# A fused attention, expert and gated-unit kernel: the attention stage issued from one table of finer steps in a new order, a shorter chain for the first expert's last rows, and an earlier first gather

## The chip, the cores and the metric

The kernel runs on one core of a Trainium2 chip. The metric is device time in microseconds (us) for one launch. Five engines work side by side, each through its own instructions in order: TensorE (PE, matrix products; its weight loads are shown apart as PEld), VectorE (DVE), ScalarE (ACT), GpSimd (POOL), and SyncE (SP), which here only issues DMA transfers. POOL and ACT issue some DMA transfers too. An engine waits on semaphores that other engines or transfers set. SBUF is the memory on the core, PSUM the one that PE writes.

## The reference

Three stages follow each other; inputs are float32.

```python
# 1 attention: a linear recurrence with a complex decay, 2 batches x 8 heads x 768 steps x 48
mag = sqrt(a_re**2 + a_im**2); scale = minimum(mag, 0.999) / (mag + 1e-6)
for t in range(S):
    S_re, S_im = (ar*S_re - ai*S_im) + outer(k_t, v_t), ar*S_im + ai*S_re
    y_t = q_t @ S_re
# 2 experts: 1536 tokens x 384, 8 experts of width 1024, each token to its best expert
e = argmax(x @ w_gate); disp[e, count[e]] = x[i]      # in token order, up to a capacity
y = relu(disp[e] @ w1[e]) @ w2[e];  out[i] = gate_w[i] * y[e, pos[i]]
# 3 gated unit of width 1536 behind an RMS norm
xn = x / rms * g;  out = (silu(xn @ w_gate) * (xn @ w_val)) @ w_out
```

## The kernel before

**Attention.** The 12 chunks of 128 time steps (6 for each batch) are called c = 0 to 11 (`LAST` = 11); two neighbouring chunks form a group gi, since their decays are worked out together. For a group, ACT and DVE turn the gates into log magnitudes and angles (`squares`, `logs_1` to `logs_4`, `angles_1` to `angles_4`), with PE summing them over time (`sums`, `angles_2`, `turns`). The logarithms and the sines need two different tables of ACT, so a table load (`ACT_TABLE_LOAD`) stands at each change. For a chunk, `decays` makes the factors `R` and sends their last row to DRAM (`ends`); `ends_in` reads it back as `re`. `scaled` multiplies keys and queries with `R` (tile `kqr`), `frame` turns them by the angle (tiles `K` and `Q`, on DVE), `flip` transposes them on PE and copies them out of PSUM (`KT`, `QT`), `scores` makes half of the heads' score matrices (`ap`) and masks them on DVE (`AT`), `end_decay` transposes `re` on PE (`rp`), `state_up` and `state` carry the recurrent state (`up`, `z`, `st`), `outputs` makes `yp` and `yT`, and `route_1` makes the rows of x and the expert logits (`xb`, `lg_all`).

**Routing.** `choice` finds the best expert, `route_2` and `route_3` a row's place in its expert (`rk`, `slot_all`), and `dispatch` is an indirect DMA from POOL that scatters 128 rows into `disp`. The first expert's input is read back before the last two chunks have been scattered: their rows are added on PE with a matrix of ones (`put`), which DVE makes from `rk` and `mine`. The result, `hi_first` and `lo_first`, feeds the first product of the experts (`hp`).

**Experts.** Weights come in 64 pieces, 8 an expert; the loop has 64 steps n, one a piece, and at step n `ahead(n)` loads piece n + 8 and splits piece n + 4 into a high and a low half (ACT `hi`, DVE `lo`). Weights of the gated unit are loaded and converted in the same loop. The dictionary `more_at` says what is issued besides at a step: the routing table's arithmetic at 1 to 9, twelve scatters of 128 table rows each into `packed` (10, 13, ..., 43), its read back into `meta_in` (46), and the first group of the gated unit: four gathers of 128 rows out of `ybuf` (50), four sums of squares on ACT (`jk`, 53 to 56), the root (57), the scaling on DVE (58), and three transposes on PE (`mxp`, 61 to 63). An expert's results go to `ybuf` at the first step of the next one.

**What sets the order.** `InOrder` wraps each engine so that instructions keep the order in which the Python code calls them. In the attention stage this order is a list of calls for the first chunk and the function `chunk` for the others. Loads of SP stand in the same order. An engine therefore waits at the first instruction that isn't ready, whatever stands behind it.

Of the kernel before, what the change touches and what calls it, by code (L numbers as in the profile page):

```python
# [43 lines left out]
def tile_kernel(ctx: ExitStack, tc: tile.TileContext, q, k, v, a_re, a_im, gates, keys, vals, wg, w1, w2, cap, m_gate, m_val, m_out, rms_g, out, dbg=None):  # L44
# [270 lines left out]
    with ExitStack() as actx:  # L315
# [36 lines left out]

        def tiles(gi):
# [12 lines left out]
        def logs_1(gi, x=ALL):  # L366
            d = gd[gi]
            ea.activation(d["tB"][:, x], d["tA"][:, x], AF.Ln)
            ea.activation(d["tA"][:, x], d["tB"][:, x], AF.Exp, scale=0.5)
            ea.activation(d["l2"][:, x], d["tA"][:, x], AF.Ln, bias=b_eps)  # L370

        def logs_2(gi, x=ALL):
            d = gd[gi]
            ev.scalar_tensor_tensor(d["tB"][:, x], d["tB"][:, x], C_MIN, d["tB"][:, x], ALU.min, ALU.add)
            ev.scalar_tensor_tensor(d["th"][:, x], d["ar"][:, x], 0.0, d["tA"][:, x], ALU.max, ALU.add)
            ev.scalar_tensor_tensor(d["l2"][:, x], d["l2"][:, x], -2.0, d["tB"][:, x], ALU.mult, ALU.add)

        def logs_3(gi, x=ALL):
            d = gd[gi]
            ea.activation(d["th"][:, x], d["th"][:, x], AF.Ln)  # L380
            ea.activation(d["th"][:, x], d["th"][:, x], AF.Exp, scale=-1.0)

        def logs_4(gi, x=ALL, e=None):
            d = gd[gi]
            (e or eg).tensor_tensor(d["th"][:, x], d["ai"][:, x], d["th"][:, x], ALU.mult)
            if 1 < gi < len(groups) - 2:
                load(gi + 2, ["g"])

        def sums(gi, js=range(GM)):
            for j in js:  # L390
                c = groups[gi][j]
                L = ps_cs.tile([P, H, D], F32, tag="cs", name=f"L_{c}")
                et.matmul(f2(L), tri, f2(gd[gi]["l2"][:, j]), start=True, stop=True)
                cd[c]["L"] = L

        def decays(gi, js=range(GM)):
            cs = [groups[gi][j] for j in js]
            for c in cs:
                R = cd[c]["R"] = ch.tile([P, 2, H, D], F32, tag="R", name=f"R_{c}", bufs=4)
                ea.activation(R[:, 0], cd[c]["L"], AF.Exp, scale=-0.5)  # L400
                ea.activation(R[:, 1], cd[c]["L"], AF.Exp, scale=0.5)
                sp.dma_start(ends[c:c + 1], R[P - 1:P, 1])

# [7 lines left out]
        def angles_1(gi, x=ALL):  # L411
            ea.activation(gd[gi]["th"][:, x], gd[gi]["th"][:, x], AF.Arctan)

        def angles_2(gi, j):
            c = groups[gi][j]
# [3 lines left out]
        def turns(gi, j):  # L419

            d, c = gd[gi], groups[gi][j]
# [8 lines left out]
        def angles_3(gi, x=ALL):  # L430
# [3 lines left out]
            ev.tensor_scalar(d["ab"][:, x].bitcast(U32), d["th"][:, x].bitcast(U32), 0x7FFFFFFF, None, ALU.bitwise_and)  # L434

        def angles_4(gi, x=ALL):
# [3 lines left out]
            ea.activation(d["rot"][:, x, :, 1], d["th"][:, x], AF.Sin, scale=-TWO_PI)  # L440
            ea.activation(d["rot"][:, x, :, 0], d["ab"][:, x], AF.Sin, scale=-TWO_PI, bias=b_hpi)

        def scaled(c):

            if c > LAST:
                return
# [16 lines left out]
        def flip(c, hh):  # L463
# [4 lines left out]
            for nm in "KQ":  # L468
# [3 lines left out]
                ea.copy(d[nm + "T"][:, 4 * hh:4 * hh + 4], tp)  # L472
# [11 lines left out]
        def end_decay(c):  # L484
            if c % NC == NC - 1:
                return
# [5 lines left out]
        def state_up(c):  # L492

            d = cd[c]
            if c % NC == NC - 1:
                return
# [3 lines left out]
            return up  # L500

        def state(c, up=None):
            d = cd[c]
            if c % NC == NC - 1:
                return
            if up is None:
                up = state_up(c)
# [7 lines left out]
            eg.tensor_tensor(ns[:, :, :D], z, d["rT"][:, :, None].to_broadcast([2 * D, H, D]), ALU.mult)  # L515
            cd[c + 1]["state"] = ns

        def outputs(c):
# [10 lines left out]
            for ps in (slice(0, 2), slice(2, 4)) if c == LAST else (slice(0, 4),):  # L529
                ea.copy(d["yT"][:, ps], yp[:, ps])  # L530

        def route_1(i, later=False):
# [8 lines left out]
            (ea.copy if i % 2 == 0 or i > LAST - 3 else ev.tensor_copy)(x_t.rearrange("p (q d) -> p q d", q=4), xb[:, :, :2 * D])  # L541
# [3 lines left out]
            if not later:  # L545
                choice(i)

        def choice(i):
            d, lg = cd[i], lg_all[:, i]
            mx = mx_all[:, i]  # L550
            ev.max(mx, lg)
# [6 lines left out]
            if i > LAST - 2:  # L558
                d["mine"] = sm.tile([P, 1], F32, tag="mine", name=f"mine_{i}", bufs=2)
                ev.tensor_scalar(d["mine"], mf, 0.0, None, ALU.is_equal)  # L560

        def route_2(i, first=False):
# [6 lines left out]
            if i > LAST - 2:  # L569
                d["put"] = inp.tile([P, GM, 2, H, D], F32, tag="g", name=f"put_{i}").rearrange("p g r h d -> p (g r h d)")[:, :W]  # L570
                ev.tensor_scalar(d["put"], iota_w, rk[:, 0:1], d["mine"], ALU.is_equal, ALU.mult)
            d["rk"] = rk
            if not first:
                route_3(i)

        def route_3(i):
            d = cd[i]
            rk, oh = d["rk"], oh_all[:, i]
# [10 lines left out]

        def dispatch(i):  # L590
            eg.indirect_dma_start(disp[:, :], bass.IndirectOffsetOnAxis(ap=slot_all[:, i:i + 1], axis=0), cd[i]["x"][:, :], None)

        LN, TRIG = "natural_log_exp_and_others", "trig_and_small"

        def chunk(c, a, l):

            if c == LAST:
                route_2(c - 1)
                dispatch(c - 1)
            end_decay(c)  # L600
            scores(c, 0)
            if c == 1:
                choice(0)
            if l is not None:
                ea.preload_act_table_set(LN)
                logs_1(l)
            elif a is not None and a > 1:
                ea.preload_act_table_set(TRIG)
                angles_1(a)
            frame(c + 1, "kr", "K2")  # L610
            state(c)
            if c + 1 in LOG:
                squares(LOG[c + 1])
            scores(c, 1)
            if 0 < c < LAST:
                route_2(c - 1)
            frame(c + 1, "qr", "Q2")
            if l is not None:
                logs_2(l)
            outputs(c)  # L620
            if a is not None:
                angles_2(a, 0)
                turns(a, 0)
                angles_2(a, 1)
            if c < LAST:
                flip(c + 1, 0)
            if l is not None:
                logs_3(l)
            elif a is not None:
                turns(a, 1)  # L630
                angles_3(a)
            route_1(c)
            if c < LAST:
                flip(c + 1, 1)
            if a is not None:
                angles_4(a)
            if l is not None:
                sums(l)
                decays(l)
                for j in groups[l]:  # L640
                    ends_in(j)
                logs_4(l)
            scaled(c + 2)
            if c < LAST:
                dispatch(c - 1)
            if c == LAST - 1:
                xd_first = inp.tile([P, GM, 2, H, D], F32, tag="kq", name="xd_first")[:, :, 0].rearrange("p g h d -> p g (h d)")
                sp.dma_start(xd_first, disp[0:W, :].rearrange("(s p) d -> p s d", p=P))
                cd[LAST]["xd"] = xd_first

        ea.preload_act_table_set(LN)
        load(0, ["g"], True)
# [39 lines left out]
        u, w = ONE  # L692
        squares(0, u, ev)
        squares(0, w)
        logs_1(0, u)
        logs_2(0, u)
        warm(9)
        sums(0, [0])
        logs_3(0, u)
        logs_4(0, u, ev)  # L700
        logs_1(0, w)
        logs_2(0, w)
        squares(1, ALL, ev)
        logs_3(0, w)
        decays(0, [0])
        logs_1(1)
        logs_4(0, w, ev)
        scaled(0)
        logs_2(1)
        ea.preload_act_table_set(TRIG)  # L710
        angles_1(0, u)
        angles_1(0, w)
        warm(27)
        angles_2(0, 0)
        angles_2(0, 1)
# [472 lines left out]
```

## Time and profile before

| what | value |
|---|---|
| runs, median (lowest to highest) | 546.01 us (544.01 to 546.9), 3 runs |
| the profiled execution's own time | 545.61 us |
| its span, first to last instruction | 543.9 us |
| PE busy | 514.0 us, 95% |
| DVE / ACT / POOL busy | 332.6 / 294.7 / 96.4 us |
| mean granted clock of PE | 0.986 of full speed |

The span is cut into stages by PE's own instructions: the first scores of chunk 1 start at 41.84 us, the first product of the experts at 160.72, the eighth expert at 286.61 and the gated unit at 311.78. A busy PE is not a PE at its peak: matmuls are pipelined and the record of one covers its passage, so that short waits can vanish in it.

### The profile page before, as it was taken

To read this page: it belongs to the slowest core of one execution; us is meant where nothing else is said; L and a number is where in the kernel's file an instruction comes from. 1 tells how busy PE (TensorE), PEld (TensorE's weight loads), DVE (VectorE), ACT (ScalarE), POOL (GpSimd) and SP (SyncE) were. 2 spreads that over 40 slices of the span, in tenths; PEclk is the share of its full clock that TensorE was granted. 3 is DMA by queue.
4 is the path that set the end of the run, shared out by engine and by line. 5 is a ranking of instruction groups with operands and counts; after the bars stand their busy time and mean duration, and the time that the engine had idled before them with its cause. 6 is when DMAs were issued, how large, how long until landed. Compare 5 with 4: busy or idle time off the path is not lost. (4 is left out here: it accounts for less than half of the span.)

```text
span 543.9 us, 8679 instructions
## 1 busy us (share of the span) xinstructions
PE 514.0 (95%) x3298; PEld 454.6 (84%) x3298; DVE 332.6 (61%) x659; ACT 294.7 (54%) x492; POOL 96.4 (18%) x147
## 2 busy tenths in 40 slices
PE   6789998999889999999999799999999999999994
PEld 2467876778779999999998788899988899888894
DVE  4749798797747989898976887751144431333300
ACT  6868697794426776777758465642223421323200
POOL 5022441633800112110020020001400001000011
PEclk9979999999999999999999899999999999999998
DMA  8175714305317989999994252310221100000000
GB/s 302 41 253 179 257 36 152 127 11 164 102 60 242 321 254 289 319 313 305 283 341 140 69 193 87 100 47 30 72 74 29 30 14 30 16 1 0 2 31 33
DMA packets 31579, 72.74 MB, mean 134 GB/s; under 512 B 6750, under 2 KB 13674, under 8 KB 31530
## 3 DMA queue, kind: packets, MB, share of 16 engines
q1 hardware_dynamic: 26538, 61.86, 35.3%
q0 software_dynamic: 2688, 7.10, 3.8%
q10 hardware_dynamic: 2304, 3.15, 1.6%
q8 instruction: 28, 0.46, 0.3%
q14 instruction: 21, 0.17, 0.1%
HBM read 59.87 MB, written 12.23 MB: 133 GB/s over the span
## 5 line engine op out<-in xcount | busy, mean ns | idle before, releaser
L58 DVE TENSOR_TENSOR sg<-vp,sg 128x512 f32<-128x512 f32 x36 | 24.9, 692 | 77.1 <-PE vp L58 75.0
L58 DVE TENSOR_TENSOR lo<-raw,hi 128x768 fp32r<-128x768 f32 x60 | 57.2, 953 | 8.1 <-ACT hi L58 7.5
L58 ACT CAST hi<-raw 128x768 fp32r<-128x768 f32 x64 | 53.2, 835 | 8.1 <-PE op L58 2.7
L58 ACT CAST uh<-sg 128x512 fp32r<-128x512 f32 x36 | 22.3, 620 | 64.8 <-DVE sg L58 60.5
L58 PE MATMUL mop<-oh__3912,uh 128*128 128x384 f32 x144 | 48.7, 338 | 0.0
L58 PE MATMUL mop<-ol__3913,uh 128*128 128x384 f32 x144 | 48.2, 335 | 0.0
L58 PE MATMUL mop<-oh__3912,ul 128*128 128x384 f32 x144 | 48.2, 334 | 0.0
L58 POOL DMA_INDIRECT out<-ot,meta_in x12 | 11.7, 976 | 202.0 <-ACT ot L58 202.0
L58 PE MATMUL op<-hi,hh 128*128 128x384 f32 x128 | 45.6, 356 | 0.0
L58 PE MATMUL op<-hi,hl 128*128 128x384 f32 x128 | 43.6, 341 | 0.2 <-DVE hl L58 0.2
L58 PE MATMUL op<-lo,hh 128*128 128x384 f32 x128 | 43.5, 340 | 0.0
L58 ACT COPY ot<-mop 128x384 f32<-128x384 f32 x12 | 5.8, 481 | 53.1 <-PE mop L58 53.1
L58 DVE TENSOR_TENSOR ul<-sg,uh 128x512 fp32r<-128x512 f32 x36 | 24.8, 689 | 11.9 <-ACT uh L58 11.9
L58 ACT ACTIVATE sg<-gp 128x512 f32<-128x512 f32 x36 | 21.5, 598 | 16.9 <-PE gp L58 16.6
L58 PE MATMUL gp<-mxh,gh 128*128 128x512 f32 x108 | 30.6, 391 | 0.0
L58 PE MATMUL gp<-mxl,gh 128*128 128x512 f32 x108 | 30.4, 389 | 0.0
L58 PE MATMUL gp<-mxh,gl 128*128 128x512 f32 x108 | 30.3, 389 | 0.0
L58 PE MATMUL vp<-mxh,vh 128*128 128x512 f32 x108 | 30.3, 389 | 0.0
L58 PE MATMUL vp<-mxl,vh 128*128 128x512 f32 x108 | 30.3, 389 | 0.0
L58 PE MATMUL vp<-mxh,vl 128*128 128x512 f32 x108 | 30.3, 389 | 0.0
L58 PE MATMUL ap<-QT,KT 96*128 96x128 f32 x192 | 28.0, 291 | 2.3 <-DVE AT L58 1.5
L58 PE MATMUL hp<-xh,hi 128*128 128x256 f32 x168 | 29.5, 283 | 0.5 <-ACT xh L58 0.5
(215 smaller groups left out, 1279.2 us busy)
## 6 DMA issues: line engine op xcount, KB each, us to landing
raw<-in_moe_w SPq DMA_DIRECT2D x64, 384.0 KB
w_g<-in_moe_w_gate SPq DMA_DIRECT2D x9, 512.0 KB
w_v<-in_moe_w_val SPq DMA_DIRECT2D x9, 512.0 KB
w_o<-in_moe_w_out SPq DMA_DIRECT2D x12, 384.0 KB
g<-in_gates SPq DMA_DIRECT2D x5, 768.0 KB
kq<-in_keys SPq DMA_DIRECT2D x5, 768.0 KB
v<-in_vals SPq DMA_DIRECT2D x12, 256.0 KB
disp<-zt SPq DMA_DIRECT2D x4, 768.0 KB
```

The source lines that it names most:

```text
L58: ins = getattr(self.eng, op)(*args, **kw)
```

## The change

The attention stage is now issued from a table, `ORDER`. A step is a name and a chunk or group (`sc.9` is `scaled` for chunk 9; `u` and `w` are the two halves of group 0); an apostrophe puts the step's work on another engine. Against before, `scaled` goes from DVE to POOL for seven chunks (0, 1, 2, 5, 6, 9, 10); four copies to `QT`, three to x and one to `yT` go from ACT to DVE; two state products and one angle product go from POOL to DVE. `act` loads a table of ACT whenever the next function needs the other one. `logs_1` to `logs_3` are cut into single instructions.

```diff
-        def chunk(c, a, l):
-
-            if c == LAST:
-                route_2(c - 1)
-                dispatch(c - 1)
-            end_decay(c)
-            scores(c, 0)
...
-        for c in range(1, B * NC):
-            chunk(c, ANG.get(c), LOG.get(c))
...
+        ORDER = """
...
+            mi.10 d.9 s0.11 s1.11 o.11
+            ch.10 rt.10 x.11' xd.0 d.10 fi.0 mi.11 pi.10 pi.11
+        """
+        for line in ORDER.strip().splitlines():
+            for step in line.split():
+                name, at = step.rstrip("'").split(".")
+                do[name](at, step.endswith("'"))
```

For the last two chunks `mine` gets the place in the first expert from the logits themselves, without the index of the best expert:

```diff
+        def mine(i):
+
+            lg, mx = lg_all[:, i], mx_all[:, i]
+            ev.max(mx, lg)
+            own = sm.tile([P, 1], BF16, tag="own", name=f"own_{i}", bufs=2)
+            ev.tensor_scalar(own, lg[:, 0:1], mx[:, 0:1], None, ALU.is_ge)
+            r0 = ps_r.tile([P, 1], F32, tag="r", name=f"r0_{i}")
+            et.matmul(r0, ones_b, acc_oh[:, 0:1], start=True, stop=False)
+            et.matmul(r0, strict, own, start=False, stop=True)
+            own_f = sm.tile([P, 1], F32, tag="own_f", name=f"own_f_{i}", bufs=2)
+            ev.tensor_copy(own_f, own)
...
+            ev.tensor_scalar(put, iota_w, r0, own_f, ALU.is_equal, ALU.mult)
```

The rest of the last chunk's routing (`choice`, `route_2`) comes behind `lo_first`. In the expert loop the gathers read only the rows of the first five experts, and the steps move:

```diff
-            return g.indirect_dma_start(y, None, ybuf[:, :], bass.IndirectOffsetOnAxis(ap=meta_in[:, i, 0:1], axis=0))
+            return g.indirect_dma_start(y, None, ybuf[:(E - 3) * W, :] if i < TG else ybuf[:, :], bass.IndirectOffsetOnAxis(ap=meta_in[:, i, 0:1], axis=0))
...
+        def first_places():
+
+            ev.tensor_scalar(meta_in[:, :TG, 0], meta_in[:, :TG, 0], (E - 3) * W - 1, None, ALU.min)
+            list(islice(early, TG))
...
-        more_at = {10 + 3 * i: partial(scatter, i) for i in range(NT)}
+        more_at = {10 + 2 * i: partial(scatter, i) for i in range(NT)}
...
-        more_at[46] = read_packed
-        for n, steps in ((50, 4), (53, 1), (54, 1), (55, 1), (56, 1), (57, 1), (58, 1), (61, 1), (62, 1), (63, 1)):
+        more_at[37] = read_packed
+        more_at[42] = first_places
+        for n, steps in ((49, 1), (50, 1), (51, 1), (52, 1), (53, 1), (54, 1), (61, 1), (62, 1), (63, 1)):
```

On PE in the first chunk, before the change, the transpose of the decay's last row (`rp`) stands between the two halves of the scores (`ap_0`, `ap_1`):

```order
L58 MATMUL L_383<-l_1_273,tri 128x384
L58 MATMUL Kp_1_388<-ident,K_0_335 96x128 x4
L58 MATMUL Qp_1_394<-ident,Q_0_337 96x128 x4
L58 MATMUL L_400<-l_1_273,tri 128x384
L58 MATMUL ap_0_431<-QT_369,KT_370 128x128 x4
L58 MATMUL up_437<-v_214,K_0_335 96x48 x8
L58 MATMUL rp_446<-ident,re_357 96x8
L58 MATMUL ap_1_455<-QT_369,KT_370 128x128 x4
```

After it, on PE in the first chunk, the same transpose stands between the first two angle sums (`TH`), ahead of the last six of the 42 filler products (`warm`):

```order
L58 MATMUL TH_327<-th_242,tri_th 128x384
L58 MATMUL rp_335<-ident,re_294 96x8
L58 MATMUL TH_339<-th_242,tri_th 128x384
L58 MATMUL L_344<-l_0_241,tri 128x384
L58 LDWEIGHTS ones_b
```

The transpose and its wait for `re` have moved ahead of the first chunk's scores.

On POOL around chunks 7 and 8 (`th` is an angle product, `st` a state, `sq` a sum of squares, `disp<-x` a dispatch), before:

```order
L58 TENSOR_TENSOR th_996<-g_674,th_996 128x768
L58 DMA disp<-x_1071,slot_all 2176x384
L58 MEMSET st_1248 96x8x16
L58 TENSOR_TENSOR st_1248<-z_1246,rT_1224 96x8x48
L58 TENSOR_TENSOR sq_1251<-sq_1251 128x2x384
L58 DMA disp<-x_1174,slot_all 2176x384
```

On POOL at the same place, after:

```order
L58 TENSOR_TENSOR th_995<-g_674,th_995 128x768
L58 MEMSET st_1255 96x8x16
L58 TENSOR_TENSOR st_1255<-z_1253,rT_1203 96x8x48
L58 TENSOR_TENSOR kqr_1280<-kq_1022,R_1249 128x768
L58 TENSOR_TENSOR sq_1288<-sq_1288 128x2x384
L58 DMA disp<-x_1037,slot_all 2176x384
```

A product `kqr` of 128x768, which was DVE's, has come in, and the dispatch stands behind it.

On ACT in the seventh expert (`yd` its results to `ybuf`, `hh` the first products' high half, `hi` a weight piece, `xh` the next expert's input), before:

```order
L58 ACTIVATE hh_3_3579<-hp_3_3552 128x512
L58 CAST xh_3585<-xp_0_3587 128x256
L58 CAST hi_3609<-raw_3462 128x768
L58 CAST gh<-wf_g_1_3412 128x512
L58 ACTIVATE jk_0_3615,ms_3516<-yt_3515,meta_in 128x384
L58 CAST xh_3585<-xp_1_3617 128x256
```

On ACT in the seventh expert, after:

```order
L58 COPY yd_3489<-op_1_3359 128x384
L58 DMA ybuf<-yd_3489 128x384
L58 ACTIVATE hh_0_3494<-hp_0_3462 128x512
L58 ACTIVATE jk_0_3498,ms_3288<-yt_3287,meta_in 128x384
L58 CAST hi_3524<-raw_3404 128x768
L58 CAST vh<-wf_v_0_3345 128x512
L58 ACTIVATE hh_1_3530<-hp_1_3500 128x512
```

The first use of a gathered tile, `jk_0`, has moved from behind the fourth `hh` of the expert to behind its first.

## Rows read from the trace of the kernel before

**Rows 1.** Busy time by stage: stretch, its length, busy of each engine, clock, DMA share, GB/s.
```profile
0.00:41.84 41.84, 32.27 (x156) 19.24 (x156) 22.74 (x39) 30.77 (x48) 10.12 (x71) 0.92 0.58 203
41.84:160.72 118.88, 109.65 (x1019) 92.81 (x1019) 95.11 (x250) 81.54 (x127) 47.91 (x39) 1.00 0.37 121
160.72:286.61 125.89, 125.52 (x887) 123.89 (x886) 110.21 (x185) 88.47 (x152) 18.80 (x17) 1.00 0.89 289
286.61:311.78 25.17, 21.34 (x133) 19.85 (x133) 19.61 (x34) 16.30 (x31) 0.00 (x0) 0.93 0.32 100
```

**Rows 2.** Timeline of PE from 30.9 us: start, us, engine, operation, idle before.
```profile
30.94 0.22 PE L58 MATMUL rp<-ident,re 8*96 8x8 f32 x1 [1.77 <-DMA re<-ends]
```

**Rows 3.** Timeline of SP's transfers from 14 us; merged rows cover several.
```profile
14.57 10.11 SPq L58 DMA_DIRECT2D ends<-R  x2
...
25.48 2.44 SPq L58 DMA_DIRECT2D re<-ends  x4
```

**Rows 4.** Busy time and clock in two stretches where the clock fell.
```profile
30.00:38.00 8.00, 7.06 (x32) 5.08 (x33) 3.92 (x6) 4.54 (x6) 1.66 (x2) 0.57 0.57 223
303.60:307.60 4.00, 4.00 (x17) 3.90 (x17) 3.96 (x8) 0.42 (x1) 0.00 (x0) 0.57 0.00 0
```

**Rows 5.** Waits of PE from 41.84 to 160.72: us in total, times, longest.
```profile
PE Qp L58 <- DVE Q L58: 2.0, 2, 1.8
PE yp L58 <- DVE end L58: 1.6, 3, 0.7
PE ap L58 <- DVE AT L58: 1.5, 6, 0.3
PE xb L58 <- ACT yT L58: 1.5, 4, 0.6
```

**Rows 6.** Timeline of DVE from 142 us: two products of one shape.
```profile
142.67 2.40 DVE L58 TENSOR_TENSOR K<-kqr,rot 128x768 f32<-128x768 f32 x1
...
146.76 0.95 DVE L58 TENSOR_TENSOR Q<-kqr,rot 128x768 f32<-128x768 f32 x1
```

**Rows 7.** Timeline of POOL from 142 us.
```profile
142.45 4.30 POOL L58 TENSOR_TENSOR lo<-raw,hi 128x768 fp32r<-128x768 f32 x2 [2.23 <-ACT hi L58]
```

**Rows 8.** Groups of DVE and of POOL, 40 to 151: busy us, mean ns, idle.
```profile
L58 DVE TENSOR_TENSOR K<-kqr,rot 128x768 f32<-128x768 f32 x10 | 11.0, 1096 | 2.5 <-ACT rot L58 2.5
L58 DVE TENSOR_TENSOR kqr<-kq,R 128x768 f32<-128x768 f32 x9 | 8.5, 950 | 0.0
...
L58 POOL TENSOR_TENSOR th<-g,th 128x768 f32<-128x768 f32 x4 | 8.0, 1997 | 26.5 <-ACT th L58 26.5
```

**Rows 9.** Timelines of DVE and PE at the end of the attention stage.
```profile
156.68 0.16 DVE L58 FIND_INDEX8 mi<-mx_all,lg_all 128x8 uint32<-128x8 f32 x1
...
157.06 0.23 DVE L58 TENSOR_SCALAR oh_all<-iota,mf 128x8 bf16<-128x8 f32 x1
...
159.51 0.70 PE L58 MATMUL xp_first_at<-put,x 128*128 128x256 f32 x2 [0.52 <-DVE put L58]
```

**Rows 10.** Waits of PE from 286 to 312.
```profile
PE mxp L58 <- issue: 3.1, 1, 3.1
PE hp L58 <- ACT xh L58: 0.5, 1, 0.5
PE op L58 <- DVE hl L58: 0.2, 1, 0.2
```

**Rows 11.** One tile (`packed`): its scatters' ns, first and last start; their landing.
```profile
L58 POOL DMA_INDIRECT packed<-meta,place x12: 966/1094/1642, 181.5 to 245.2; - x12
...
DMA to landing us min/median/max: 4.2/5.3/7.3
```

**Rows 12.** Timelines of SP, POOL and ACT around the first gather.
```profile
264.44 0.39 SPq L58 DMA_DIRECT2D meta_in<-packed  x1
...
279.45 0.99 POOL L58 DMA_INDIRECT yt<-ybuf,meta_in  x1 [33.09 <-DMA raw<-in_moe_w]
...
284.34 0.62 ACT L58 ACTIVATE jk<-yt,meta_in 128x384 f32<-128x384 f32 x1 [4.47 <-DMA yt<-ybuf,meta_in]
```

More of the change, by code (lines that the diff above doesn't have):

```diff
@@ L351, in tile_kernel, with act @@
         ONE = [slice(j, j + 1) for j in range(GM)]
+        LN, TRIG = "natural_log_exp_and_others", "trig_and_small"
+        table = [None]
+        def act(need, out, x, func, **kw):
+            if table[0] != need:
+                ea.preload_act_table_set(need)
+                table[0] = need
+            ea.activation(out, x, func, **kw)
         def tiles(gi):
@@ L385, in logs_4, with sums, decays @@
             (e or eg).tensor_tensor(d["th"][:, x], d["ai"][:, x], d["th"][:, x], ALU.mult)
[L386 to L402, printed above, removed]
+        def sums(c):
+            gi, j = group_of[c]
+            L = cd[c]["L"] = ps_cs.tile([P, H, D], F32, tag="cs", name=f"L_{c}")
+            et.matmul(f2(L), tri, f2(gd[gi]["l2"][:, j]), start=True, stop=True)
+        def decays(c):
+            R = cd[c]["R"] = ch.tile([P, 2, H, D], F32, tag="R", name=f"R_{c}", bufs=4)
+            act(LN, R[:, 0], cd[c]["L"], AF.Exp, scale=-0.5)
+            act(LN, R[:, 1], cd[c]["L"], AF.Exp, scale=0.5)
+            sp.dma_start(ends[c:c + 1], R[P - 1:P, 1])
         def ends_in(c):
@@ L439, in angles_4, with scaled @@
                 d["rot"] = tmp.tile([P, GM, H, 2, D], F32, tag="rot", name=f"rot_{gi}", bufs=2)
[L440 to L446, printed above, removed]
+            act(TRIG, d["rot"][:, x, :, 1], d["th"][:, x], AF.Sin, scale=-TWO_PI)
+            act(TRIG, d["rot"][:, x, :, 0], d["ab"][:, x], AF.Sin, scale=-TWO_PI, bias=b_hpi)
+        def scaled(c, e=None):
             d = cd[c]
@@ L471, in flip @@
                     et.transpose(tp[:, h], d[nm + "2"][:, 4 * hh + h].rearrange("p j d -> p (j d)"), ident)
-                ea.copy(d[nm + "T"][:, 4 * hh:4 * hh + 4], tp)
+                (e.tensor_copy if e is not None and nm == "Q" else ea.copy)(d[nm + "T"][:, 4 * hh:4 * hh + 4], tp)
         def scores(c, hh):
@@ L588, in route_3, with first_in @@
             ev.tensor_tensor(acc_oh, acc_oh, oh, ALU.add)
+        first, xps = [], []
+        def first_in():
+            first.extend(wsp.tile([P, KD, W], F32R, tag=tg, name=f"{tg}_first", bufs=LS + 1) for tg in ("hi", "lo"))
+            xps.extend(p.tile([P, W], F32, tag=tg, name=f"xp_first_{tg}") for p, tg in ((ps_at, "at"), (ps_cs, "cs"), (ps_cs, "cs")))
+            for kk in range(KD):
+                for t in range(2):
+                    et.matmul(xps[kk][:, t * P:(t + 1) * P], cd[LAST]["xd"][:, t, kk * P:(kk + 1) * P], ident, start=t == 0, stop=False)
@@ L590, in dispatch, with put_in @@
+        def put_in(c):
+            for kk in range(KD):
+                et.matmul(xps[kk], cd[c]["x"][:, kk * P:(kk + 1) * P], cd[c]["put"], start=False, stop=c == LAST)
         def dispatch(i):
             eg.indirect_dma_start(disp[:, :], bass.IndirectOffsetOnAxis(ap=slot_all[:, i:i + 1], axis=0), cd[i]["x"][:, :], None)
-        LN, TRIG = "natural_log_exp_and_others", "trig_and_small"
-        def chunk(c, a, l):
-            if c == LAST:
-                route_2(c - 1)
-                dispatch(c - 1)
-            end_decay(c)
-            scores(c, 0)
[L602 to L649, printed above, removed]
@@ new lines, in xd_in, with of_group, of_group_on @@
+        def xd_in():
+            xd = cd[LAST]["xd"] = inp.tile([P, GM, 2, H, D], F32, tag="kq", name="xd_first")[:, :, 0].rearrange("p g h d -> p g (h d)")
+            sp.dma_start(xd, disp[0:W, :].rearrange("(s p) d -> p s d", p=P))
+        def of_group(f, *more, **kw):
+            return lambda at, o: f(int(at[0]), {"u": ONE[0], "w": ONE[1]}.get(at[1:], ALL), *more, **kw)
+        def of_group_on(f, usual, other):
+            return lambda at, o: f(int(at[0]), {"u": ONE[0], "w": ONE[1]}.get(at[1:], ALL), other if o else usual)
@@ L651, in tile_kernel @@
         ea.preload_act_table_set(LN)
+        table[0] = LN
         load(0, ["g"], True)
@@ L712, in tile_kernel @@
[L712 to L715, printed above, removed]
-        turns(0, 0)
-        angles_3(0, u)
-        angles_4(0, u)
-        ea.preload_act_table_set(LN)
-        frame(0, "kr", "K2")
-        frame(0, "qr", "Q2")
-        warm(6)
-        turns(0, 1)
-        angles_3(0, w)
-        sums(0, [1])
-        decays(0, [1])
-        zero(0)
-        ends_in(0)
-        ends_in(1)
-        load(2, ["g"])
-        scaled(1)
-        warm(0)
-        flip(0, 0)
@@ L734, in tile_kernel @@
-        sums(1, [0])
-        logs_3(1)
-        logs_4(1, ALL, ev)
-        flip(0, 1)
-        sums(1, [1])
-        decays(1)
-        ends_in(2)
-        ends_in(3)
-        for z in (1, 2, 3, 4):
-            zero(z)
-        load(2, ["v"])
-        load(3, ["g"])
-        ea.preload_act_table_set(TRIG)
-        angles_4(0, w)
-        angles_1(1)
-        scores(0, 0)
-        up = state_up(0)
-        end_decay(0)
-        state(0, up)
-        scores(0, 1)
-        outputs(0)
-        squares(2)
@@ L782, in tile_kernel @@
-        xd_first = cd[LAST]["xd"]
-        first = [wsp.tile([P, KD, W], F32R, tag=tg, name=f"{tg}_first", bufs=LS + 1) for tg in ("hi", "lo")]
-        xps = [p.tile([P, W], F32, tag=tg, name=f"xp_first_{tg}") for p, tg in ((ps_at, "at"), (ps_y, "y"), (ps_u, "u"))]
-        for kk in range(KD):
-            for t in range(2):
-                et.matmul(xps[kk][:, t * P:(t + 1) * P], xd_first[:, t, kk * P:(kk + 1) * P], ident, start=t == 0, stop=False)
-        def put_in(kk, c):
-            et.matmul(xps[kk], cd[c]["x"][:, kk * P:(kk + 1) * P], cd[c]["put"], start=False, stop=c == LAST)
@@ L800, in tile_kernel @@
+        """
[3 more added lines that the diff above has]
+                do[name](at, step.endswith("'"))
+        for kk in range(KD):
+            ea.copy(first[0][:, kk], xps[kk])
+            ev.tensor_tensor(first[1][:, kk], xps[kk], first[0][:, kk], ALU.subtract)
+        choice(LAST)
+        route_2(LAST)
         dispatch(LAST)
```

181 lines of the change are left out of this document (74 added, 107 removed).

## The prediction

> **What bounds the kernel now.** I cut the span into stages first [rows 1]. From 160.72 to 286.61 us PE is busy 125.52 of 125.89 us, so a change in the order of other engines can win nothing there. Three stretches are open: the start (PE busy 32.27 of 41.84), the chunks with the tail (109.65 of 118.88) and the eighth expert (21.34 of 25.17). In the chunks PE comes nearest to being the bound: DVE has 95.11 us of work there, ACT 81.54, POOL 47.91. PE's idle time is the most that the records show to be won, and 109.65 a floor that is a little too high, since records of pipelined matmuls also cover short waits. Then I read who PE waits for in each stretch, and where its clock falls.
>
> **Start.** PE stands 1.77 us for `re`, the decay's last row that comes back from DRAM [rows 2]. The row was sent at 14.57, yet its read was issued at 25.48 [rows 3]: SP had the second chunk's row and a zero fill ahead of it. Behind this wait the granted clock averages 0.57 from 30 to 38 us [rows 4], that is, mostly at the lower level, 1.2 instead of 2.4 GHz; 8 x 0.43 = 3.4 us of full speed are missing. The most to win is 1.77 + 3.4 = 5.2 us. After the change the read follows the first chunk's row directly, and `rp` runs at PE's first angle sums, behind which six filler products still stand: some ten microseconds early, so the read has 4 to 5 us to land. Late next is the second half of `rot` and the arctangent of group 1 on ACT, which have the same table loads ahead of them as before. I take 4.0 of the 5.2. Ends: 0 (the angles' chain on ACT decides, and the clock falls again) and -5.2.
>
> **Chunks.** PE is idle for 118.88 - 109.65 = 9.2 us in this stretch [rows 1]; the largest waits are for DVE's `Q` (2.0), a DVE instruction ahead of `yp` (1.6), `AT` (1.5) and `yT` (1.5) [rows 5]. Finer steps let `K`, `Q` and the masks stand further ahead of their use, and no table load is added. Moved work: `scaled` on DVE costs 0.950 us, so seven of them free 6.7 us; in return DVE gets four `QT`, three x and one `yT` copies (about 0.55 each by DVE's and ACT's own copies in the trace, 4.4 us in all) and three products of some 0.5 to 1 us, so its sum stays near 95 us and well under PE's. POOL gets seven products at about 2.0 us [rows 8], 14 us, and gives up about 4. I take half of the idle time, 4.6 us, since several waits come from chains and not from the order alone. One end is -9.2.
>
> The other end comes from a clash in the trace. `K` lasts 2.40 us beside a POOL product that began 0.22 us before it, and the next product of that shape 0.95 us [rows 6, 7]: 1.45 us lost by waiting for POOL. If each of the seven new POOL products held up one DVE product so, and all of it reached PE, that would be 7 x 1.45 = +10.2 us. I stay with -4.6 because POOL's products already run beside `K` there, and the mean of ten `K` is 1.096 us [rows 8], 0.146 above the free 0.95: one hit of 1.45 in ten. Both ends go into the range.
>
> The Trainium skill ("SBUF — State Buffer", section "SBUF: two separate sides") states why: GpSimd and VectorE share one port pair as an exclusive lock, so that a VectorE instruction with two SBUF inputs and a GpSimd one that reads SBUF fully block each other. The 2.40 against 0.95 us agrees. By that rule every new POOL product is a possible block, and moving work from DVE to POOL wins less than DVE's freed time; by the idle rows alone it wins half of what is open. The rule speaks against this part of the change and is carried below as a rival.
>
> **Tail.** In the trace the last rows' `put` is waited for 0.52 us [rows 9] and the first `hp` starts at 160.72 [rows 1]. `mine` takes index, cast, one-hot and flag (156.68 to about 157.35) off this chain and adds a comparison, a cast and, ahead of them on DVE, the copy of x. PE's twelve transposes and six `put` products remain in series, so at most about 0.8 us goes. In return, `rk`'s last product now stands between the fourth and the fifth `hp`, behind an index chain that begins only after the three `lo_first`: 157.29 - 156.68 = 0.6 us from index to one-hot [rows 9]. The two cancel: 0, with ends -0.8 and +0.7.
>
> **Gated unit's first gather.** In the eighth expert PE waits 3.1 + 0.5 + 0.2 = 3.8 us [rows 10], and at 303.6 to 307.6 the clock averages 0.57, which costs 4 x 0.43 = 1.7 us [rows 4]. Together 5.5. The chain is visible: the gather starts at 279.45, ACT stands 4.47 us at `jk` until the rows have landed [rows 12], all copies behind `jk` slip, DVE follows, and PE starves at `mxp` 15 us later. One step is 125.89 / 56 = 2.25 us [rows 1]. Step 50 began at 160.72 + 50 x 2.25 = 273.2, so the gather came 6.3 us after its step. Step 42 is 255.2 on the same scale; with the same delay the gathers start at 261.5, the first lands 4.9 us later (284.34 - 279.45) at 266.4, and the fourth some 4 us after that. `jk` at step 49 comes at 271.0, the fourth at 277.7: no wait. Late next is only PE's own work. I take -5.5, with ends 0 and -5.5.
>
> The read of the table is now at step 37, or 160.72 + 83.2 = 243.9. The scatters hang on one another, so that the rule for their steps changes nothing: the twelfth begins at 245.2 and lands some 5.3 us later, 250.5 [rows 11]. SP therefore stands about 6.6 us, with the loads of pieces 45 to 47 behind it. A piece is read four steps, 9 us, after its load's step, and its split has four more steps before PE needs it. I put 0 in the sum; the end is +3 (6.6 less a cushion of some 4). The new limit on DVE at step 42 (255.2) finds `meta_in` landed since about 253 to 255, so DVE barely waits.
>
> **Sum.** -4.0 - 4.6 + 0 - 5.5 + 0 = -14.1. The profiled execution took 545.61 us in all, 0.4 below the median of 546.01 shown: 545.6 - 14.1 = 531.5.
>
> **Rivals.**
> 1. The port clash eats the chunks' gain. For it: rows 6 and 7; against it: half as many free DVE microseconds would do to leave PE the bound. Only start and gather remain: 545.6 - 9.5 = 536.1 us.
> 2. The gather's wait changes place. SP's hold drains the loads (DMA is busy 0.89 of the expert stretch [rows 1], so it catches up slowly), ACT waits for pieces, and DVE, busy 110.21 of 125.89, cannot make it up. Against it: 9 us of lead. Then 545.6 - 8.6 = 537.0, or 540 with the full 3 us.
> 3. Slower: the lock in the chunk stretch, at its full price. Seven hits of 1.45 us that all reach PE, +10.2, while the start gains nothing because its angle chain on ACT decides: 545.6 + 10.2 - 5.5 = 550.3. It decides from the point where the hits exceed start and gather together, 9.5 / 1.45, or 7 more hits with a start that gains. Against it: only about one `K` in ten is hit now [rows 8].
> 4. The order takes out nearly all idle time: 545.6 - 5.2 - 9.2 - 0.8 - 5.5 = 524.9, and less where records hid waits.
>
> **How the numbers follow.** Forecast 0.60, rivals 0.16, 0.09, 0.10 and 0.05. About 0.5%, 2.7 us, can be told from no change here: below 543.3 is faster, above 548.7 slower. Of the second rival and of the first a tenth to a fifth lies within no change, of the third a fifth; so faster 0.86, same 0.06, slower 0.08. The likeliest case has a range of its own of 525 to 538. The range of eight in ten reaches from 522 (a little under rival 4) to 542.5 (past rivals 1 and 2), and leaves out rival 3 and the far side of 4.
>
> **What would show it.** Start: no wait at `rp`, the first scores of chunk 1 near 38 us, and a clock near 1.0 from 28 to 38. Chunks: first `hp` near 152, PE idle about 4 to 5 us between them; more `K`, `Q` or `oh_all` far above their usual duration would speak for rivals 1 and 3. Gather: no wait at `jk`, none of 3 us at `mxp`, clock 1.0, and the last expert in about 19.5 us. A wait of SP near 7 us ahead of `meta_in` with no wait of ACT for pieces would confirm the zero. I am wrong if the stage from 160 to 286 gets longer, or if the first `hp` comes later than 157.

## The result: slower, where faster was forecast

| | before | after |
|---|---|---|
| median (lowest to highest), runs | 545.08 us (544.01 to 546.9), 4 | 553.84 us (549.62 to 554.25), 4 |
| ratio, 95% interval | | 1.0142 (1.0100 to 1.0184) |
| profiled execution, its span | 545.61, 543.9 us | 554.25, 552.4 us |
| PE / DVE / ACT / POOL busy | 514.0 / 332.6 / 294.7 / 96.4 us | 518.2 / 344.4 / 289.7 / 106.4 us |
| mean granted clock of PE | 0.986 | 0.970 |

The forecast of 531.5 us and its range, 522 to 542.5, are both missed. The spans differ by 8.5 us. The stages of after, cut at the same instructions as in [rows 1] (stretch, length, busy of PE, PEld, DVE, ACT, POOL, clock, DMA share, GB/s):

```profile
0.00:36.07 36.07, 29.55 (x155) 17.16 (x156) 22.47 (x38) 28.36 (x45) 14.79 (x73) 1.00 0.68 228
36.07:170.25 134.18, 118.08 (x1023) 102.43 (x1021) 107.78 (x257) 80.14 (x123) 49.95 (x42) 0.90 0.32 109
170.25:300.81 130.56, 126.75 (x886) 125.30 (x887) 112.17 (x193) 92.62 (x160) 22.02 (x17) 0.99 0.86 281
300.81:319.80 18.99, 18.57 (x133) 18.18 (x133) 17.09 (x27) 11.19 (x19) 0.00 (x0) 1.00 0.41 122
```

Against [rows 1] the start is 5.8 us shorter, the chunks with the tail 15.3 longer, the first seven experts 4.7 longer, the eighth 6.2 shorter; the gated unit is 0.5 longer. The sum is +8.5. Of the 15.3 us, 6.9 are more idle time of PE (134.18 - 118.08 = 16.10, before 9.23) and 8.4 are the same products lasting longer: the clock averages 0.90 where it was 1.00.

**The chunks.** PE's largest waits there (us in total, times, longest), to be read beside those of [rows 5]:

```profile
PE yp L58 <- DVE AT L58: 5.2, 3, 2.3
PE up L58 <- ACT x L58: 4.6, 1, 4.6
PE ap L58 <- DVE rT L58: 1.3, 1, 1.3
```

All three lead to DVE. In its timeline (start, us, operation), as in [rows 6], some instructions last several times as long as others of their shape:

```profile
71.92 2.57 DVE L58 TENSOR_TENSOR K<-kqr,rot 128x768 f32<-128x768 f32 x1 [1.62 <-POOL kqr L58]
...
128.59 5.50 DVE L58 TENSOR_SCALAR ab<-th 128x768 uint32<-128x768 uint32 x1
...
149.34 3.31 DVE L58 TENSOR_TENSOR kqr<-kq,R 128x768 f32<-128x768 f32 x1
```

POOL at the same moments, as in [rows 7]:

```profile
70.06 3.61 POOL L58 TENSOR_TENSOR kqr<-kq,R 128x768 f32<-128x768 f32 x2
...
128.34 1.81 POOL L58 TENSOR_TENSOR kqr<-kq,R 128x768 f32<-128x768 f32 x1
130.12 3.55 POOL L58 TENSOR_TENSOR lo<-raw,hi 128x768 fp32r<-128x768 f32 x2
...
148.96 1.02 POOL L58 DMA_INDIRECT disp<-x,slot_all  x1 [0.16 <-DVE oh_all L58]
150.01 1.82 POOL L58 TENSOR_TENSOR lo<-raw,hi 128x768 fp32r<-128x768 f32 x1
```

`ab` usually takes 0.56 us. It began 0.25 us after `kqr` and ended at 134.09, 0.4 us after the last of three POOL products in a row (133.67): it waited for the whole row. `kqr` at 149.34 ended 0.8 us after a dispatch and the `lo` behind it. `K` first waited 1.62 us for its own `kqr`, began as POOL's next one did, and ended at 74.49, 0.8 us after that one (73.67). How one such hit reaches PE, in ACT's and PE's timelines:

```profile
134.22 0.48 ACT L58 COPY x<-xb 128x384 f32<-128x384 f32 x1 [5.30 <-DVE lg_all L58]
```

```profile
134.75 2.79 PE L58 MATMUL up<-v,K 128*96 128x48 f32 x16 [4.58 <-ACT x L58]
```

Behind `ab` stands `lg_all`, behind that ACT's copy of x, behind that PE's `up`. Then the clock (window, length, busy, clock):

```profile
128.00:136.00 8.00, 3.42 (x28) 3.21 (x26) 7.53 (x9) 2.69 (x5) 6.20 (x5) 0.87 0.23 74
136.00:144.00 8.00, 8.00 (x55) 7.40 (x55) 3.05 (x5) 0.85 (x2) 1.47 (x1) 0.50 0.17 51
```

For 8 us after the wait PE runs at 0.50, the 1.2 GHz level. The wait of 4.6 us costs some 4 us again. The means per group on DVE from 40 to 151 us (busy us, mean ns), against [rows 8], where `K` had 1096 and `kqr` 950:

```profile
L58 DVE TENSOR_TENSOR K<-kqr,rot 128x768 f32<-128x768 f32 x9 | 11.7, 1296 | 2.3 <-POOL kqr L58 1.6 <-ACT rot L58 0.7
...
L58 DVE TENSOR_TENSOR kqr<-kq,R 128x768 f32<-128x768 f32 x5 | 8.4, 1682 | 0.0
L58 DVE TENSOR_SCALAR ab<-th 128x768 uint32<-128x768 uint32 x4 | 7.3, 1829 | 0.1
```

Summed over the stretch, the DVE instructions that last over 0.3 us more than is usual for their shape are ten and lose 17.4 us; before they were five and lost 7.4. This sum is called the held-up time below. Three of the five before are `oh_all`, which otherwise takes 0.23 us. In DVE's and POOL's timelines of before:

```profile
52.35 1.67 DVE L58 TENSOR_SCALAR oh_all<-iota,mf 128x8 bf16<-128x8 f32 x1
```

```profile
52.17 1.82 POOL L58 TENSOR_TENSOR th<-g,th 128x768 f32<-128x768 f32 x1 [4.84 <-ACT th L58]
```

Not every hit lasts up to the end of POOL's row. The `K` of [rows 6, 7] ended at 145.07, while the row of two ran to 146.75. It got in after the first `lo`, and the second lasted 2.53 us where the first took 1.80 (POOL's timeline of before):

```profile
144.22 2.53 POOL L58 TENSOR_TENSOR lo<-raw,hi 128x768 fp32r<-128x768 f32 x1
```

The traces of the five runs in the old order below show the same. Why `K` got in there and `ab` did not is open.

**The experts.** SP's transfers, as in [rows 12], then PE's product that waits for one of them, then the two windows behind it:

```profile
249.69 2.16 SPq L58 DMA_DIRECT2D raw<-in_moe_w  x2
260.39 0.38 SPq L58 DMA_DIRECT2D meta_in<-packed  x1
...
263.34 0.61 SPq L58 DMA_DIRECT2D xd<-disp  x1
```

```profile
272.49 0.41 PE L58 MATMUL xp<-ident,xd 128*128 128x128 f32 x2 [3.48 <-DMA xd<-disp]
```

```profile
268.00:272.00 4.00, 1.01 (x9) 0.80 (x7) 2.99 (x6) 2.90 (x5) 0.00 (x0) 1.00 1.04 405
272.00:276.00 4.00, 3.52 (x17) 3.46 (x17) 3.96 (x7) 2.69 (x5) 2.06 (x2) 0.73 1.03 406
```

SP issues nothing from 251.85 to 260.39, since the read of the table waits for the last scatter (SP's waits: us, times, longest):

```profile
SPq L58 <- DMA packed<-meta,place: 8.5, 1, 8.5
```

The next expert's input, `xd`, stands behind it, is issued at 263.34 and lands after PE wants it; PE waits 3.48 us and is at 0.73 after that. Weight pieces came late as well. ACT stood 3.19 us for one (its timeline) and 1.08 for another, but PE went on beside that until `xd`:

```profile
266.47 0.60 ACT L58 ACTIVATE hh<-hp 128x512 fp32r<-128x512 f32 x1 [3.19 <-DMA raw<-in_moe_w]
```

### The profile page after: what moved, and what is told of

The parts are those of the page before. It is cut to its first block, busy times and chain, and to the rows that moved or that the text cites. A ratio compares the mean times of both kernels' runs of the same rounds, so it can differ in the third digit from the quotient of the medians.

```text
span 552.4 us, 8690 instructions
## 1 busy us (share of the span) xinstructions
PE 518.2 (94%) x3302; PEld 462.0 (84%) x3302; DVE 344.4 (62%) x666; ACT 289.7 (52%) x484; POOL 106.4 (19%) x151
## 5 line engine op out<-in xcount | busy, mean ns | idle before, releaser
L58 ACT ACTIVATE sg<-gp 128x512 f32<-128x512 f32 x36 | 21.5, 598 | 16.8 <-PE gp L58 16.6
L58 POOL DMA_INDIRECT packed<-meta,place x12 | 16.2, 1351 | 70.0 <-DMA packed<-meta,place 52.5
L58 PE MATMUL hp<-xl,hi 128*128 128x256 f32 x168 | 29.3, 283 | 0.0
```

The costliest lines, as they stand in the source:

```text
L58: ins = getattr(self.eng, op)(*args, **kw)
```

## The experiments

Medians are compared with the kernel before, run on the same chip beside them: 545.18 us (31 runs) for the first four kernels, 544.13 (12) for `lo` alone and the last three, 544.74 (31) for the other four. The changed kernel has the four runs above, beside 545.08. A chunk stretch runs from the first scores of chunk 1 to the first `hp`.

**One part undone: `kqr` on DVE.** In the table each `sc.N'` becomes `sc.N`:

```diff
-            ... n1.0u R.0 sc.0' m0.0w ...
+            ... n1.0u R.0 sc.0 m0.0w ...
```

> The changed kernel with one thing undone: all seven products kqr that went to POOL stand on DVE again, at the same places of the table. Theory (the lock): the ten DVE instructions that lasted 17.4 us above their usual time in the chunk stretch (5 with 7.4 before) lose most of this, the 5.50 us for one ab goes, and with the stalls most of the 8.5 us that PE's products lasted longer at the lower clock. DVE gets 7 x 0.95 = 6.7 us of work back. Chunk stretch from 134.2 to some 120 to 124 us, median 541 to 545. Rival (the order itself: chains and placement starve PE, the lock is a side matter): chunk stretch stays at 131 to 138, median 551 to 558, since DVE has even more to do.

Measured 546.6 us (544.35 to 551.14, 10 runs), ratio to before 1.0032 (0.9998 to 1.0065), 7.2 below the changed kernel. Its chunk stretch, with the clock behind the five busy times:

```profile
37.73:161.63 123.90, 110.65 (x1024) 95.72 (x1022) 106.11 (x261) 79.96 (x123) 43.49 (x36) 0.97 0.34 117
```

10.3 us shorter than after, though DVE has more to do there (261 instructions, 257 in after). Held-up time 12.2 us. One `ab` is still held, now by the two `lo` alone, which end at 127.71 (DVE's timeline):

```profile
124.32 3.96 DVE L58 TENSOR_SCALAR ab<-th 128x768 uint32<-128x768 uint32 x1
```

The stretch fell into the theory's range, and the order as sole cause is refuted. But the median is 1.6 us above that range, and only 5.2 of the 17.4 us held up are gone, not most of them. Up to 1.6 us of the gain is not the lock but `K`'s wait for a `kqr` that POOL made late.

**That part alone, in the old order.**

```diff
-            ev.tensor_tensor(f4(kq), f4(gd[gi]["kq"][:, j]), f4(d["R"]), ALU.mult)
+            (eg if c in (0, 1, 2, 5, 6, 9, 10) else ev).tensor_tensor(f4(kq), f4(gd[gi]["kq"][:, j]), f4(d["R"]), ALU.mult)
```

> The kernel before with that one part alone: scaled of chunks 0, 1, 2, 5, 6, 9, 10 on POOL, all else in the old order. Theory (the lock): more DVE instructions last far above their usual time, and PE stands for them; chunk stretch 3 to 15 us longer, median 548 to 560, with the granted clock below 1.0 somewhere between 42 and 160. Rival (the order): DVE gets 6.7 us free, the stretch stays within 2 us of 118.9, median 543 to 547.

Measured 552.46 us (549.02 to 554.01, 10 runs), ratio 1.0113 (1.0082 to 1.0144): seven products moved off DVE make the kernel 7.3 us slower, as the theory said. The chunk stretch is 124.60 us, 5.7 longer than before; held-up time is 13.1 us. The worst hit is on an instruction of one element a partition. The timelines of DVE, POOL and PE, then the window of the eight microseconds from 84:

```profile
80.64 3.95 DVE L58 SCALAR_TENSOR_TENSOR slot_all<-slf_all,over,spare 128x1 int32<-128x1 f32 x1
```

```profile
80.22 0.84 POOL L58 TENSOR_TENSOR st<-z,rT 96x384 f32<-96x384 f32 x1
81.00 1.81 POOL L58 TENSOR_TENSOR sq<-sq 128x768 f32<-128x768 f32 x1
82.77 1.80 POOL L58 TENSOR_TENSOR kqr<-kq,R 128x768 f32<-128x768 f32 x1
```

```profile
85.59 1.09 PE L58 MATMUL Qp<-ident,Q 128*96 128x128 f32 x4 [2.52 <-DVE Q L58]
```

```profile
84.00:92.00 8.00, 6.37 (x25) 5.25 (x26) 5.14 (x14) 1.86 (x4) 1.58 (x2) 0.57 0.44 173
```

`slot_all`, which otherwise takes 0.22 us, ends at 84.59 with POOL's row of three (84.57). Its price is set by POOL's row, not by its own size.

**The gather's edits alone, in the old order** (the diff is the last one of the change, above).

> The kernel before with the gather's edits alone (scatters every second step, table read at 37, places and gathers at 42, uses from 49). Theory (SP's hold): the read holds SP 7 to 9 us, the load of the seventh expert's input is late, PE stands some 3.5 us for xd and its clock falls after that; this pays back what the missing waits at jk and mxp give (5.5): median 543.5 to 547. Rival (the hold came only because the attention stage was late): no wait for xd, all of the 5.5 is won, median 539 to 541.

Measured 546.26 us (542.38 to 548.86, 10 runs), ratio 1.0012 (0.9977 to 1.0047): nothing won. SP issues nothing from 244.30 to 252.77, 8.5 us (SP's timeline), and PE waits for `xd` (us, times, longest):

```profile
243.97 0.33 SPq L58 DMA_DIRECT2D raw<-in_moe_w  x1
252.77 0.38 SPq L58 DMA_DIRECT2D meta_in<-packed  x1
```

```profile
PE xp L58 <- DMA xd<-disp: 3.2, 1, 3.2
```

The hold belongs to the edit, not to a late attention stage.

**The start's edit alone.**

```diff
         scaled(0)
+        zero(0)
+        ends_in(0)
...
         angles_3(0, u)
+        end_decay(0)
...
-        zero(0)
-        ends_in(0)
...
-        end_decay(0)
```

> The kernel before with the start's edit alone: the decay's last row of chunk 0 is read back right behind one zero fill, and rp stands behind the first angle sums. Theory: the start's gain is real and independent of the table: no wait at rp, the first scores of chunk 1 some 4 to 5.8 us earlier than 41.84, median 539.5 to 542. Rival: the wait only moves (to the sines of group 0 or the states), the first scores stay after 40, median 543.5 to 546.

Measured 544.57 us (542.58 to 546.99, 10 runs), ratio 0.9984 (0.9955 to 1.0012). The wait at `rp` is gone, the clock from 30 to 38 us is 1.00, and the first scores of chunk 1 come earlier by 2.2 us (PE's timeline; before 41.84), less than the theory said:

```profile
39.64 1.16 PE L58 MATMUL ap<-QT,KT 96*128 96x128 f32 x8
```

The clock now falls earlier, from 20 to 30 us, behind a wait of 2.8 us for an angle that ACT makes; before, that wait is 2.5 us and the clock 1.00. Later PE waits 1.1 us for another angle. The 2.2 us that are won last up to the scores of chunk 9. Then the clock falls from 130 to 140 us, where it was 1.00 before, and only 0.8 is left at the first `hp` (159.88). The two windows:

```profile
20.00:30.00 10.00, 9.91 (x52) 6.02 (x51) 7.26 (x12) 7.24 (x13) 0.00 (x0) 0.83 0.12 26
130.00:140.00 10.00, 7.94 (x70) 6.94 (x69) 6.33 (x17) 4.84 (x9) 6.16 (x5) 0.83 0.31 100
```

PE's wait for `Q` there is 1.8 us in both kernels, so the trace doesn't tie this second fall to the edit. In the run with start and gather and the read at 41, below, the clock stays at 1.00 there, and the first `hp` comes at 158.42, 2.3 us before 160.72. The median lies in the rival's range and can't be told from before.

**`kqr` and `lo` on DVE.** As the first experiment, and each `p.N` of the table (the split of a weight piece) becomes `p.N'`, which puts `lo` on DVE.

> The changed kernel with the seven kqr products and also the four low halves lo of the first weight pieces on DVE: POOL keeps dispatches, states, sums of squares. Theory (the lock): the ab of 3.96 us, the kqr of 3.30 and the oh_all of 1.87 that were left beside lo in the run with kqr alone go back to 0.56, 0.95 and 0.23; DVE gains 7.3 us and pays 4 x 0.95 = 3.8; the wait of 3.5 at up and the clock of 0.83 from 120 to 140 go. Median 538 to 543 after 546.6. Rival (what is left comes from the order): 545 to 549, with the wait at up still there.

Measured 543.33 us (538.79 to 544.83, 10 runs), ratio 0.9972 (0.9938 to 1.0006). Held-up time 4.9 us; `ab`, `kqr` and `oh_all` past 124 us are at their usual durations, PE's wait at `up` is down to 1.8 us but not gone, and the clock of the chunk stretch is 1.00:

```profile
37.73:156.60 118.87, 107.81 (x1024) 92.81 (x1022) 102.17 (x265) 80.00 (x123) 37.58 (x32) 1.00 0.36 122
```

All of the 15.3 us is gone in this execution; the median is 0.3 us above the theory's range. But 118.87 is what the old order had (118.88), so the trace shows no gain of the finer steps in the chunks. The old order had `lo` on POOL; it was not tried with `lo` on DVE.

**`lo` alone on DVE**, `kqr` left on POOL.

> The changed kernel with only the four low halves lo of the first weight pieces on DVE; the seven kqr stay on POOL. Theory (a held-up DVE instruction waits for a whole row of POOL products, so the row counts, not the single product): ab near 128 has one kqr of 1.81 us beside it in place of a row of 5.3 us, lasts some 2.2 in place of 5.50; kqr of 3.31 and oh_all of 1.87 near 147 to 153 go back to 0.95 and 0.23; DVE gains 7.3, pays 3.8; the clock of 0.5 to 0.73 from 132 to 144 and 152 to 156 rises. Median 546 to 550. Rival (the seven kqr are the whole harm, the pairs of lo stood there before too): 552 to 555.

Measured 550.07 us (548.28 to 551.77, 4 runs), ratio 1.0122 (1.0082 to 1.0162), just above the theory's range. `ab` has one `kqr` beside it (130.30 to 132.11) and ends 0.43 us after it (DVE's timeline):

```profile
131.34 1.20 DVE L58 TENSOR_SCALAR ab<-th 128x768 uint32<-128x768 uint32 x1
```

The chunk stretch is 125.1 us. Alone, `kqr` on DVE takes 10.3 us off it and `lo` 9.1, together 15.3, since both had a part in the row around 128. A second loss is of `kqr` alone, the row of two at 70: from the first scores of chunk 4 to those of chunk 5 it takes 16.6 us in after, 16.9 here, 12.4 with `kqr` on DVE and 10.5 before.

**Fillers in the waits.** The changed kernel with POOL's products left where they are; the fillers write to a bank that is free there:

```diff
-            ed.4 sq.4 z.4' o.4 ...
+            ed.4 sq.4 z.4' W.9 o.4 ...
-            ed.9 up.9 s1.9 ...
+            ed.9 W.18 up.9 s1.9 ...
-            ed.10 s1.10 Q.11 pl.6 o.10 ...
+            ed.10 s1.10 Q.11 pl.6 W.9 o.10 ...
```

> The changed kernel with filler products added where PE waits in the chunk stretch: 18 ahead of up in chunk 9, 9 ahead of yp in chunks 4 and 10 (0.21 us each at 2.4 GHz); nothing else is changed and the fillers' result is not used. The waits themselves stay. Theory (the lower clock behind a wait costs again what the wait cost): clock near 1.0 from 74 to 84 and 130 to 160, PE's products some 5 us shorter in all, median 547 to 551. Rival (other engines set the pace there, the clock is without effect): median 552.5 to 556.

Measured 545.1 us (544.31 to 546.43, 10 runs), ratio 0.9999 (0.9970 to 1.0028): 8.7 us less than the changed kernel by the medians, some 8 by the ratios, and more than expected, by 36 products that compute nothing. `ab` is held as long as ever, and so are the others (17.4 us in all); only the clock differs. DVE's `ab`, PE's fillers with the `up` behind them, and the window of the chunk stretch:

```profile
125.45 5.51 DVE L58 TENSOR_SCALAR ab<-th 128x768 uint32<-128x768 uint32 x1
```

```profile
126.96 4.06 PE L58 MATMUL warm_n<-zt,ones_b 128*128 128x512 bf16 x18
131.62 1.56 PE L58 MATMUL up<-v,K 128*96 128x48 f32 x16 [0.60 <-ACT x L58]
```

```profile
35.69:161.20 125.51, 116.67 (x1059) 97.66 (x1057) 107.84 (x257) 79.87 (x123) 49.99 (x42) 0.99 0.34 117
```

`up` takes 1.56 us in place of 2.79. The stretch is 8.7 us shorter than after: the clock behind the waits cost more than the waits added (6.9).

**The read of the table at step 41.** On top of `kqr` and `lo` on DVE:

```diff
-        more_at[37] = read_packed
+        more_at[41] = read_packed
```

> As the run with kqr and lo on DVE, and the table's read at step 41 instead of 37, so that SP comes to it some 9 us later, when the twelfth scatter has landed. Theory (SP's hold): no gap of SP ahead of meta_in, no wait for xd, clock 1.0 from 260 to 280, no new wait at jk or mxp: 3.5 + about 1.5 = 5 us below the run with the read at 37, median 533 to 538. Rival (a later read makes gathers and uses late again): the wait for xd goes but one of 3 us at mxp comes back, 538 to 542.

Measured 540.44 us (539.0 to 545.61, 10 runs), ratio 0.9936 (0.9907 to 0.9965): 2.9 below the read at 37, less than expected. SP stands 2.2 us in place of 7.7, and nothing waits for `xd`; but now DVE waits, at the limit on the places in step 42, and PE 4.3 us behind it (in the profile, which is the slowest of these runs):

```profile
262.61 0.17 DVE L58 TENSOR_SCALAR meta_in<-meta_in 128x4 int32<-128x4 int32 x1 [4.26 <-DMA meta_in<-packed]
```

**Start and gather in the old order, read at 41.**

> The kernel before with the start's edit and the gather's edits, the table read at 41. Theory (SP's hold was all that paid the gather's gain back): no wait for xd, jk or mxp, clock 1.0 from 260 to 310, 544.6 - 5 = 539.6, median 537.5 to 541.5. Rival (the expert stretch is bound by its loads, so the last expert waits whatever the gather does): 543 to 546.

Measured 541.85 us (539.46 to 543.04, 10 runs), ratio 0.9944 (0.9915 to 0.9973), between the two theories: no wait for `xd` and none of 3 us at `mxp`, but DVE stands 2.13 us for `meta_in` here too.

**Gathers at 44, in the table and in the old order.**

```diff
-        more_at[42] = first_places
+        more_at[44] = first_places
```

> The changed kernel with kqr and lo on DVE, the table's read at step 41 and the gathers at 44 in place of 42, so that DVE does not stand for meta_in (4.26 us in the profile of the run with read at 41, 4.3 us of PE behind it). Theory: no wait at xd, xp, jk, mxp in the experts; the clock 1.0 from 240 to 310; median 535 to 539, the lowest so far. Rival (gathers at 44 come too late for their uses from 49): a wait at jk and mxp of 2 to 4 us, 539 to 543.

> The kernel before, in its old order of the attention stage, with the start's edit, the gather's edits, the read at 41 and the gathers at 44. Theory: the waits of 0.8 + 0.8 us behind xl and DVE's 2.13 us at meta_in go, 1 to 2 us below the 541.85 of the run with gathers at 42: 539.5 to 541. Rival (they were hidden, or a later gather costs as much): 541.5 to 543.5. Against the table with all on DVE: if the table is lower by over 1 us, its finer order is worth something once POOL is out of it.

The table: 539.46 us (536.0 to 541.17, 7 runs), ratio 0.9906 (0.9868 to 0.9944). The old order: 538.76 us (537.8 to 541.38, 6 runs), ratio 0.9916 (0.9886 to 0.9946). The table's is just above the theory's range, the old order's just below. All eight experts, of the old order first, then of the table:

```profile
159.80:305.00 145.20, 144.41 (x1020) 142.18 (x1019) 129.46 (x219) 104.61 (x181) 18.41 (x17) 1.00 0.84 268
```

```profile
161.80:306.90 145.10, 143.98 (x1018) 141.98 (x1019) 128.77 (x219) 103.25 (x179) 17.99 (x17) 1.00 0.84 268
```

Before they took 125.89 + 25.17 = 151.06 us. The gather's gain is 5.9 us once SP's stand is down to some 2 us and DVE doesn't wait for the table. The two medians lie 0.7 us apart with overlapping intervals, so the finer order shows no worth of its own, though its start is 1.9 us shorter (first scores of chunk 1 at 37.7 against 39.6). In this profile of the table the clock fell from 120 to 140 us to 0.83, and its chunk stretch is 124.12 us, for the same code that took 118.87 in one execution and 122.7 in the run with the read at 41. The old order has 118.9 to 120.3 in its five traces with `kqr` on DVE.

**Table and fillers together** (8 ahead of `up` in chunk 9, 3 ahead of `yp` in chunk 4, 3 between the scores of chunk 10).

> As the run with read at 41 and gathers at 44, with 14 filler products more where PE still waits in the chunks (8 ahead of up in chunk 9, 3 ahead of yp in chunk 4, 3 between the halves of the scores of chunk 10). Theory (the clock falls behind such waits in part of the executions): median 1 to 3 us below the run without fillers and a narrower spread, 533.5 to 537. Rival (the waits left are too short for the clock): the same within 1 us, or 1 to 3 us slower by the fillers' own 3 us.

Measured 536.01 us (535.42 to 540.53, 6 runs), ratio 0.9854 (0.9825 to 0.9882): the fastest, 1.5% faster than before and, by the two ratios, 2.8% faster than the changed kernel (0.9854 / 1.0142 = 0.972). It lies 3.4 us below the table without these fillers, but the two intervals overlap a little. Five of its six runs lie within 1.3 us; the profiled one is the sixth, so its trace doesn't show where the rest is won. In it PE waits 3.2 us for an earlier `xd`, issued at 231.12 with no hold of SP, at a DMA share of 0.96 to 1.06: an `xd` can also be late without the hold. That fillers in the old order would do as much wasn't tried.

## Why the prediction was wrong, step by step

- **Start**, -4.0 (0 to -5.2): measured -5.8, past the end. Right in sign, but the working was not: the read of `re` alone brings 2.2 us, not 4.0. The clock fell earlier instead (0.17 of 10 us, 1.7 us) and PE waited 1.1 us for an angle, both of which the prediction had only in its zero end. What remained came from the table's order of the first chunk (37.73 with `kqr` on DVE) and from its `kqr` on POOL (36.07).
- **Chunks**, -4.6: measured +15.3, past the end of +10.2. This is the step that failed, at the sentence "I stay with -4.6 because POOL's products already run beside `K` there, and the mean of ten `K` is 1.096 us". Three things were wrong in it. `K` is not the only instruction that can be held: `ab`, `kqr`, `oh_all` and `slot_all` were, and the mean of ten `K` hid that the trace of before already had five hits, three of them on `oh_all`. A hit need not end with one product, 1.45 us over: `ab`, `oh_all` and `slot_all` stood up to the end of POOL's row, `ab` 4.9 us over, and the new `kqr` made such rows longer. And at its worst PE was to lose what DVE loses. The added held-up time is 10.0 us; that this is near the 10.2 is luck, since it comes from other instructions and longer hits. Behind PE's waits the clock fell as well, and with fillers in the waits the stretch is 8.7 us shorter. The Trainium skill ("SBUF — State Buffer", section "SBUF: two separate sides"), weighed and set aside in the prediction, was right about the block. It has the lock held for one instruction; `K` of [rows 6, 7], which got in after the first of two products, agrees with that, while `ab` at 128.59 got in only when POOL's row of three was over.
- **Half of the idle time** as the order's gain: with POOL out of it the stretch is 118.87 us against 118.88, and in two other executions 122.7 and 124.12. No gain is shown.
- **Tail**, 0 (-0.8 to +0.7): from the last scores (159.52) to the first `hp` (170.25) it takes 10.7 us, before 160.72 - 150.53 = 10.2. Right in size, +0.5 inside the chunks' figure, but not by its terms: PE's wait for `put` is gone and it doesn't wait at `rk`; instead the first `hp` waits 0.9 us for `lo_first`, which no term had.
- **Gather**, -5.5: the eighth expert is 6.2 us shorter, no wait at `jk`, 0.4 us at `mxp`, and 5.9 us are won where nothing pays it back. Right.
- **SP's hold**, 0 (end +3): the hold was forecast at 6.6 us and was 8.5; its price was 4.7 us, past the end (in the old order 150.02 - 145.20 = 4.8). The cushion was counted for weight pieces alone, and ACT stood for those too, 3.19 and 1.08 us; but PE waited for the expert's input `xd`, which stands in the same queue with less lead, and again the clock added to the wait. Rival 2 named the hold and ACT's waits, not `xd`, and had it at 3.
- **Rival 3** (the lock at full price) is nearest to what happened, with the start gaining all the same. It had 0.10. By its own rule it decides once the hits exceed start and gather; that the hits would come with a loss of clock was in no term.

Put together: -5.8 + 15.3 + 4.7 - 6.2 + 0.5 = 8.5 us, as measured.

## What to carry to other kernels

Before work goes from DVE to POOL, look in POOL's timeline for what will then stand back to back: a DVE instruction that is caught can wait for the end of the row, even a tiny one (`slot_all`, 3.95 us), though `K` in [rows 6, 7] did not. Price a new wait of PE twice, once as idle time and once at the clock that the trace shows after such waits; fillers in the wait are the cheap test of the second half. When a read that waits for others moves up in a shared queue, look for the transfer behind it with the least lead, not for the typical one.

## What was not expected of the hardware

- An instruction of one element a partition (`slot_all`) lasted 3.95 us beside three POOL products, and ended with the last of them.
- 36 products without use made a kernel 8.7 us faster, with the same waits of DVE.
- The same attention code took 118.87 us in one execution (clock 1.00 from 120 to 160), 122.7 in a second (0.91) and 124.12 in a third (0.83, then 0.91). What decides between them is open.
- A `K` caught by two POOL products got in between them, where `ab` had to wait for all three. Why is open.
